# Token mixes from one shared difference, ten plain-float32 attention heads instead of twelve, and a first q that ScalarE loads and rounds

## The chip, the cores and the metric

The kernel runs on one core of a Trainium2 chip. The metric is the device time of one execution in microseconds (us); lower is better. The engines are called PE (TensorE matmuls), PEld (TensorE weight loads), DVE (VectorE), ACT (ScalarE), POOL (GpSimd) and SP (SyncE, which here issues the DMAs).

## What the kernel computes

Four sequences ("batches") of 448 tokens with 12 heads of 64 channels go through sigmoid attention, a gated layer that mixes each token with the one before it, and a token and channel mixer. Everything is float32.

```python
scores = scale * q @ k.T - log(S);  attn = sigmoid(scores);  x = attn @ v          # per batch and head
x_prev = x shifted by one token (zeros first)
xk = mu_k * x + (1 - mu_k) * x_prev;   xr = mu_r * x + (1 - mu_r) * x_prev
k = relu(xk @ w_k);   v = k*k @ w_v;   r = sigmoid(xr @ w_r);   x = r * v
h = relu(x.T @ w_tok1) @ w_tok2;       u = x + h.T
out = u + relu(u @ w_ch1) @ w_ch2
```

## The kernel before

**Precision.** A float32 matrix is split into a high part, rounded to the fast format float32r, and a low part, the rest (`split`, L97 to L102): one cast on ACT or DVE (L99 or L101) and one subtract, always on DVE (L102). A product of two split matrices is three matmuls, L409, L411 and L412 of `products`. An attention head multiplies its scores with v either split or plain. A split head has, for each half of its scores `a`, a cast `ah` on ACT (L211) and subtracts on DVE (L215 for the first half, L217 and L218 for the second), then 7 matmuls (L235, L237), an ACT copy (L239) and a DVE add (L240) into `xe`; its v is split too. A plain head has 4 matmuls in plain float32 (L230, recorded as 8) and one ACT copy (L231), and nothing on DVE. `NATIVE` (L51) names the plain heads as (batch, head): 8 of batch 0, 4 of batch 1.

**The mix.** `xe` holds x with a column of zeros ahead, channels on partitions, in six blocks of 128 channels by 448 tokens. `mix_unit` does one block for one of the two mixes: x_prev times (1 - mu) (L396 on ACT, or L398 on DVE for batch 2), mu times x plus that (L399 on DVE), and a split of the result into `Ah` and `Al`. Which engine takes a cast is in `ONDVE` (L38).

**The stages.** Batch 0's attention runs first. Then `first_part(b)` runs for batch 0 (products with w_r, six column blocks; with w_k, eight; with w_v, six of two chunks each; then the token mixer), with the attention of batch 1 spread between its matmuls, then `first_part` of batch 1, then `second_part` for both (w_ch1, w_ch2). The same again for batches 2 and 3. Weights arrive in a raw 8-byte format on their first use (L308), are narrowed by two ACT (L273, L275) and two DVE instructions (L278, L281), stored (L322), and split into `whi` (ACT, L99) and `wlo` (DVE, L102); a matmul chunk can't start its L412 before its `wlo`. On later uses they are loaded narrowed. Raw tiles have 2 buffers, split weights 3, PSUM tiles of the products 3.

**Order.** The work is written out in units (attention, mixes, weights), but a scheduler at build time sets the order on each engine; each engine then runs its own list strictly in that order. The very first loads are issued by SP (`load_k`, `load_q`, `load_v`), and the first head's q is split by DVE.

Of the kernel before, what the change touches and what calls it, by code (L numbers as in the profile page):

```python
# [22 lines left out]
P = 128  # L23
NT = C // P
# [10 lines left out]
    return ap.bitcast(F32)  # L35


ONDVE = [('K', 0), ('K', 1), ('K', 2), ('K', 3), ('Q', 0), ('Q', 2), ('Q', 3), ('V', 1), ('V', 2), ('kk', 0), ('kk', 3), ('mix', 1), ('mix', 2), ('mix', 3), ('prev', 2), ('sq', 2)]  # L38


WARM = 12
# [6 lines left out]

NATIVE = {(0, 1), (0, 7), (0, 4), (1, 1), (0, 3), (1, 8), (1, 4), (0, 6), (0, 2), (0, 5), (1, 9), (0, 11)}  # L51


def native(b, pr, h):
# [4 lines left out]
def kernel(  # L59
# [34 lines left out]
    def ENG(kind, b):  # L94
        return DVE if (kind, b) in ONDVE else ACT

# [12 lines left out]
    def load_k(g):  # L109
        if g < B * NPAIR:  # L110
            kns[g] = a2.tile([P, 4 * P], F32, tag="kn", name="kn")
            SP.dma_start(out=kns[g], in_=k[g])

    def load_q(g):
        if g < B * H:
            qns[g] = a3.tile([P, S], F32, tag="qn", name="qn")
            SP.dma_start(out=qns[g], in_=q[g])

    def load_v(g):
        if g < B * NPAIR:  # L120
            vns[g] = a2.tile([P, 2, 4, D], F32, tag="vn", name="vn")
            SP.dma_start(out=vns[g], in_=v[g])


    warm = const.tile([P, 1], F32, tag="warm", name="warm")
    DVE.memset(warm, 0.0)
# [5 lines left out]
    for _ in range(WARM):  # L132
        PE.matmul(idle[:, :S], zero[:, :P], zero, start=True, stop=True)

    load_k(0)
    load_q(0)
    load_v(0)
    load_q(1)

# [4 lines left out]
    load_q(2)  # L144
    load_v(1)

    mus = {}
    for name, src in (("k", mu_k), ("r", mu_r)):
        m = const.tile([P, NT], F32, tag="mu" + name, name="mu" + name)
        SP.dma_start(out=m, in_=src)  # L150
        om = const.tile([P, NT], F32, tag="om" + name, name="om" + name)
        DVE.tensor_scalar(out=om, in0=m, scalar1=-1.0, scalar2=1.0, op0=ALU.mult, op1=ALU.add)
        mus[name] = (m, om)


    xe = big.tile([P, NT, 1 + S], F32, tag="xe", name="xe")
# [15 lines left out]
    def unit_q(b, pr, h):  # L172
        g = b * NPAIR + pr
        st = att[(b, pr, h)]
        qn = qns.pop(2 * g + h)
        Q1 = a2.tile([P, S], F32R, tag="Q1", name="Q1")
        Q2 = a2.tile([P, S], F32R, tag="Q2", name="Q2")
        split(Q1, Q2, qn, ENG("Q", b))
        st["Q"] = (Q1, Q2)
        load_q(2 * g + h + 3)  # L180
        vn = vns[g][:, h]
        if native(b, pr, h):
            st["v"] = vn
        else:
            vs = a3.tile([P, 4, 2 * D], F32R, tag="vs", name="vs")
            split(vs[:, :, 0:D], vs[:, :, D:], vn, ENG("V", b))
            st["v"] = vs
        if h == 1:
            load_v(g + 2)
# [198 lines left out]
    def col(p, t):  # L388
        return p[:, t * S : (t + 1) * S]

    def mix_unit(name, t, dst, b):
        m, om = mus[name]
        t1 = tmps.tile([P, S], F32, tag="tmp", name="mix1")
        t2 = tmps.tile([P, S], F32, tag="tmp", name="mix2")
        if ENG("prev", b) is ACT:
            ACT.activation(t1, xe[:, t, 0:S], AF.Copy, scale=om[:, t : t + 1])  # L396
        else:
            DVE.tensor_scalar(out=t1, in0=xe[:, t, 0:S], scalar1=om[:, t : t + 1], scalar2=None, op0=ALU.mult)  # L398
        DVE.scalar_tensor_tensor(  # L399
            out=t2, in0=xe[:, t, 1:], scalar=m[:, t : t + 1], in1=t1, op0=ALU.mult, op1=ALU.add  # L400
        )
        split(col(dst[0], t), col(dst[1], t), t2, ENG("mix", b))


    def products(ps, n, count, parts, stacked=None):
# [19 lines left out]
    def new_mm():  # L425
        return ps_mm.tile([P, 512], F32, tag="mm", name="psmm")

    def first_part(b, xr, xk, rows, u):
        rows[:] = [big.tile([P, S], F32, tag="r%d" % m, name="r%d" % m) for m in range(NT)]


        for m in range(NT):
            ps = new_mm()
            yield from products(ps, S, NT, chunked(1, NT, xr))
            ACT.activation(rows[m], ps[:, :S], AF.Sigmoid)


        kk = pair_tiles("M", 12 * S)
        for m in range(F // P):
            ps = new_mm()  # L440
            yield from products(ps, S, NT, chunked(1, NT, xk))
            t1 = tmps.tile([P, S], F32, tag="tmp", name="k1")
            t2 = tmps.tile([P, S], F32, tag="tmp", name="k2")
            ACT.activation(t1, ps[:, :S], AF.Relu)
            if ENG("sq", b) is ACT:
                ACT.activation(t2, t1, AF.Square)
            else:
                DVE.tensor_tensor(out=t2, in0=t1, in1=t1, op=ALU.mult)
            split(col(kk[0], m), col(kk[1], m), t2, ENG("kk", b))

        yt = xk_tiles()
        ytv = [t.rearrange("p (r c) -> p r c", r=4) for t in yt]

        def y_transpose(m):
            ps = new_mm()
            psv = ps.rearrange("p (r c) -> p r c", r=4)
            ms = slice(m * P, (m + 1) * P)
            for r in range(4):  # L460
                n = P if r < 3 else TAIL
                PE.transpose(psv[:n, r], rows[m][:, r * P : r * P + n], ident)  # L462
            hi, lo = (t[:, :, ms] for t in ytv)
            split(hi[:, :3], lo[:, :3], psv[:, :3], ACT)
            split(hi[:TAIL, 3], hi[TAIL:, 3], psv[:TAIL, 3], ACT)

        for m in range(NT):
            ps = new_mm()
            for i, cost in enumerate(products(ps, S, 8, chunked(2, 4, kk))):
                yield cost  # L470
                if i == 1 and m:
                    y_transpose(m - 1)
            DVE.tensor_tensor(out=rows[m], in0=rows[m], in1=ps[:, :S], op=ALU.mult)


        h1v = [t[:, : 2 * C].rearrange("p (j c) -> p j c", j=2) for t in pair_tiles("M", 12 * S)]
        wt1 = []
        for half in range(2):
            cs = slice(half * HC, (half + 1) * HC)
            for j in range(TOK // P):  # L480
                if half == 0:
                    wt1.append(weights())
                    wst["hold"] = j == 1
                wh, wl = wt1[j]
                ps = new_mm()
                yield from products(ps, HC, 4, [(wh[:, r], wl[:, r], *(t[:, r, cs] for t in ytv)) for r in range(4)], 3)
                if half == 0 and j == 0:
                    y_transpose(NT - 1)
                ACT.activation(h1v[0][:, j, cs], ps[:, :HC], AF.Relu)
                DVE.scalar_tensor_tensor(  # L490
                    out=h1v[1][:, j, cs],
                    in0=ps[:, :HC],
                    scalar=0.0,
                    in1=f32(h1v[0][:, j, cs]),
                    op0=ALU.max,
                    op1=ALU.subtract,
                )
        wst["hold"] = False
        w_tick()
        if b % 2:  # L500
            u[:] = u_tiles()
        for m in range(NT):
            ps = new_mm()
            ms = slice(m * P, (m + 1) * P)
            yield from products(
                ps, S, 2, ((h1v[0][:, j, ms], h1v[1][:, j, ms], wt2h[:, j], wt2l[:, j]) for j in range(2))
            )
            DVE.tensor_tensor(out=rows[m], in0=rows[m], in1=ps[:, :S], op=ALU.add)
            if b % 2 == 0:
                SP.dma_start(out=away[m], in_=rows[m])  # L510
            else:
                t1 = tmps.tile([P, S], F32, tag="tmp", name="back")
                SP.dma_start(out=t1, in_=away[m])
                split(u[0][:, m, :S], u[1][:, m, :S], t1, ACT)
                split(u[0][:, m, S:], u[1][:, m, S:], rows[m], ACT)
# [39 lines left out]
                    SP.dma_start(out=out[b0 + 1, m * P : (m + 1) * P], in_=rows[m])  # L555


    def mix_units(name, box, b):
        def mix(t):
            if t == 0:  # L560
                box[name] = xk_tiles() if name == "k" else xr_tiles()
            mix_unit(name, t, box[name], b)

        return [lambda t=t: mix(t) for t in range(NT)]

    box = {}
    for i, unit in enumerate(attention_units(0, [mix_units("r", box, 0), mix_units("k", box, 0)])):
        unit()
        if i == TOK2:
            load_tok2()  # L570
            w_raw(1)
        if i == EARLY:
            w_ready(1)
# [6 lines left out]
    def spread(units, start, end):  # L580
        return [(start + (end - start) * i / len(units), f) for i, f in enumerate(units)]

    now, todo = 0.0, []
    rows, u = [], []

    def run(gen):
# [6 lines left out]
    for b in range(0, B, 2):  # L593
        nxt = {}
        todo += spread(attention_units(b + 1, [mix_units("r", nxt, b + 1)]), now, now + END_1 * t_a)
        run(first_part(b, box["r"], box["k"], rows, u))
        todo += spread(mix_units("k", nxt, b + 1), now + 0.01 * t_a, now + 0.12 * t_a)
        box = {}
        if b + 2 < B:
# [3 lines left out]
            todo += spread(mix_units("k", box, b + 2), t0 + 0.87 * t_c, t0 + 0.97 * t_c)  # L603

        def second_batch():
            while "r" not in nxt or "k" not in nxt:
                todo.pop(0)[1]()
            yield from first_part(b + 1, nxt["r"], nxt["k"], rows, u)

        run(second_batch())  # L610
        run(second_part(b, rows, u))
# [77 lines left out]
```

## Time and profile before

| | before |
|---|---|
| median of 3 runs | 942.76 us (942.66 to 944.78) |
| the profiled execution | 942.98 us, span 941.1 us |
| PE, PEld busy | 930.5 us (99%), 806.3 us (86%) |
| DVE, ACT busy | 661.2 us (70%), 517.3 us (55%) |
| granted TensorE clock, mean | 0.998 |

Busy shares are averages over the whole span; the stages differ. Matmuls are pipelined and their ends are modelled, so two matmul rows overlap by more than half their length: what one costs is the distance from its start to the next start. To a smaller extent this holds for the other engines too.

### The profile page before, as it was taken

The page shows a single profiled execution, that of the slowest core. Times are in us where ns is not written, and L with a number is a line of the kernel's source. Part 1 is how long each engine was busy: PE and PEld are TensorE (multiplying, and loading weights), DVE is VectorE, ACT ScalarE, POOL GpSimd, SP SyncE. Part 2 cuts the span into 40 slices and gives each one's busy share as a digit, 9 for nine tenths or more (in the row PEclk, how much of TensorE's full clock was granted, in tenths as well). Part 3 has the DMA queues.
Part 4 walks back from the last instruction along what each step waited for, and adds up shares of the span by engine and source line. Part 5 has one row for each costly group of instructions (what it writes and reads, how often), then busy time and mean ns, then how long its engine had stood idle before and what let it go on. Part 6 is the DMA issues. An engine that isn't in the chain of part 4 may idle for free.

```text
span 941.1 us, 12125 instructions
## 1 busy us (share of the span) xinstructions
PE 930.5 (99%) x4472; PEld 806.3 (86%) x4472; DVE 661.2 (70%) x1111; ACT 517.3 (55%) x794; POOL 1.2 (0%) x8
## 2 busy tenths in 40 slices
PE   8999999999999999999999999999999999999998
PEld 4476788779998988998988999999999998889987
DVE  8999899989567988777789478988745552323231
ACT  6998989674774767546641367767444342112210
POOL 0000000000000000000000000000000000000000
PEclk9999999999999999999999999999999999999999
DMA  7646665775344465555544333323334321232131
GB/s 240 219 134 235 233 222 192 229 231 167 118 134 139 131 223 202 194 186 185 188 144 157 123 109 116 109 63 99 106 106 151 115 80 51 90 124 71 51 110 62
DMA packets 57083, 137.38 MB, mean 146 GB/s; under 512 B 6592, under 2 KB 23488, under 8 KB 57024
## 3 DMA queue, kind: packets, MB, share of 16 engines
q1 hardware_dynamic: 57024, 136.61, 44.9%
q8 instruction: 35, 0.57, 0.3%
q14 instruction: 24, 0.20, 0.1%
HBM read 106.96 MB, written 29.62 MB: 145 GB/s over the span
## 4 chain that ended last, share of the span: by engine, by line
PE 90%; DVE 4%; DMA 3%; ACT 2%; issue 0%; SPq 0%; ACTq 0%; DVEq 0%
PE psmm L412 25%; PE psmm L409 25%; PE psmm L411 25%; PE psc L197 3%; PE psc L198 3%; PE pav L230 3%; PE pav L235 3%; PE pav L237 2%; DMA raw<-in_moe_w_k_dram 1%; PE psmm L462 1%; DVE wd L278 1%; ACT wd L273 1%; DMA raw<-in_moe_w_r_dram 1%; DMA w<-wd 1%; DVE KK L102 0%
## 5 line engine op out<-in xcount | busy, mean ns | idle before, releaser
L409 PE MATMUL psmm<-Ah,whi 128*128 128x448 f32 (+2 forms) x688 | 250.0, 364 | 1.9 <-ACT whi L99 1.9
L412 PE MATMUL psmm<-Ah,wlo 128*128 128x448 f32 (+2 forms) x688 | 250.9, 365 | 0.6 <-DVE wlo L102 0.6
L99 ACT CAST whi<-wd 128x768 fp32r<-128x768 f32 (+1 forms) x160 | 121.4, 759 | 225.0 <-PE psmm L411 204.8
L411 PE MATMUL psmm<-Al,whi 128*128 128x448 f32 (+2 forms) x672 | 244.7, 364 | 0.1
L102 DVE TENSOR_TENSOR wlo<-wd,whi 128x768 fp32r<-128x768 f32 (+1 forms) x160 | 137.8, 862 | 93.8 <-ACT whi L99 88.8
L409 PE MATMUL psmm<-Mh,whi 128*128 128x448 f32 (+2 forms) x480 | 176.4, 368 | 0.2 <-ACT whi L99 0.2
L412 PE MATMUL psmm<-Mh,wlo 128*128 128x448 f32 (+2 forms) x480 | 176.0, 367 | 0.0
L411 PE MATMUL psmm<-Ml,whi 128*128 128x448 f32 (+2 forms) x480 | 175.1, 365 | 0.0
L409 PEld LDWEIGHTS psmm<-Ah,whi 128*128 128x128 f32 x688 | 129.6, 188 | 18.3 <-ACT whi L99 2.7
L412 PEld LDWEIGHTS psmm<-Ah,wlo 128*128 128x128 f32 x688 | 129.5, 188 | 14.4 <-DVE wlo L102 2.0
L411 PEld LDWEIGHTS psmm<-Al,whi 128*128 128x128 f32 x672 | 126.4, 188 | 12.7 <-DVE Al L102 0.6
L204 ACT ACTIVATE a<-psc 128x896 f32<-128x896 f32 x96 | 87.2, 917 | 32.0 <-PE psc L198 30.4
L412 PEld LDWEIGHTS psmm<-Mh,wlo 128*128 128x128 f32 x480 | 90.1, 188 | 11.8 <-DVE wlo L102 1.6
L409 PEld LDWEIGHTS psmm<-Mh,whi 128*128 128x128 f32 x480 | 90.2, 188 | 11.0 <-ACT whi L99 0.8
L411 PEld LDWEIGHTS psmm<-Ml,whi 128*128 128x128 f32 x480 | 90.2, 188 | 8.8
L197 PE MATMUL psc<-Q,KK 128*128 128x448 f32 x192 | 71.9, 375 | 0.4 <-ACT a L204 0.4
L198 PE MATMUL psc<-Q,KK 128*128 128x448 f32 x192 | 70.6, 369 | 0.7 <-DVE Q L102 0.7
L211 ACT CAST ah<-a 128x896 fp32r<-128x896 f32 x72 | 67.7, 944 | 1.0
L278 DVE SCALAR_TENSOR_TENSOR wd<-wd,raw 128x768 uint32<-128x768 uint32 (+2 forms) x54 | 47.1, 874 | 16.4 <-ACT wd L273 8.6
L273 ACT ACTIVATE wd<-raw 128x768 f32<-128x768 f32 (+2 forms) x54 | 45.1, 835 | 24.3 <-DVE wlo L102 10.4
L536 DVE SCALAR_TENSOR_TENSOR Ml<-psmm,Mh 128x512 fp32r<-128x512 f32 (+1 forms) x48 | 29.8, 621 | 34.7 <-ACT Mh L535 34.6
L235 PE MATMUL pav<-ah,vs 128*128 128x448 f32 x144 | 53.3, 370 | 0.0
(79 smaller groups left out, 1051.6 us busy)
## 6 DMA issues: line engine op xcount, KB each, us to landing
wd<-w SPq DMA_DIRECT2D x66, 384.0 KB, 3.0
raw<-in_moe_w_ch_dram SPq DMA_DIRECT2D x24, 768.0 KB, 4.8
w<-wd SPq DMA_DIRECT2D x38, 384.0 KB, 2.6
qn<-in_q_dram SPq DMA_DIRECT2D x48, 224.0 KB, 2.9
wd<-w SPq DMA_DIRECT2D x42, 256.0 KB, 2.7
kn<-in_k_dram SPq DMA_DIRECT2D x24, 256.0 KB, 2.9
vn<-in_v_dram SPq DMA_DIRECT2D x24, 256.0 KB, 3.1
raw<-in_moe_w_k_dram SPq DMA_DIRECT2D x8, 768.0 KB, 5.6
```

The lines of the kernel that those rows point to most:

```text
L99: ACT.copy(hi, src)
L102: DVE.tensor_tensor(out=lo, in0=src, in1=f32(hi), op=ALU.subtract)
L197: PE.matmul(ps[:, j, :S], K[:, c * P : (c + 1) * P], Q1, start=True, stop=False)
L198: PE.matmul(ps[:, j, :S], K[:, c * P : (c + 1) * P], Q2, start=False, stop=True)
L204: ACT.activation(a, ps[:, :, :S], AF.Sigmoid, bias=-math.log(S), scale=1.0 / math.sqrt(D))
L211: ACT.copy(ah, a)
L235: PE.matmul(ps[:, :S], vs[:, c], ah[:, c % 2], start=(c == 0), stop=(c == 3))
L273: ACT.activation(f32(dst), f32(hi), AF.Copy, scale=2.0**-112)
L278: DVE.scalar_tensor_tensor(out=dst, in0=dst, scalar=3, in1=lo, op0=ALU.logical_shift_left, op1=ALU.bitwise_or)
L409: PE.matmul(ps[:, :n], wh, xh, start=(i == 0), stop=False)
L411: PE.matmul(ps[:, :n], wh, xl, start=False, stop=False)
L412: PE.matmul(ps[:, :n], wl, xh, start=False, stop=(i == count - 1))
```

## The change

Three edits. (1) `NATIVE` loses heads (1, 1) and (0, 11), which become split heads. (2) `mix_r` forms one difference x - x_prev per block on DVE; then two DVE instructions add (mu - 1) times it to x, once for r into a temporary and once for k, in place in `xe`; each is split as before. ACT's scaled copies (L396) are gone, and with them L398. Batch 1's cast of the mixed block goes from DVE to ACT. Batch 0's k splits become units of their own that are written into the beginning of `first_part(0)`. (3) The first q is loaded by an ACT-issued DMA, placed with the first k ahead of the warm-up, and its cast goes from DVE to ACT.

```diff
-ONDVE = [... ('mix', 1), ('mix', 2), ('mix', 3), ('prev', 2), ('sq', 2)]
+ONDVE = [... ('mix', 2), ('mix', 3), ('sq', 2)]
-NATIVE = {(0, 1), (0, 7), (0, 4), (1, 1), (0, 3), (1, 8), (1, 4), (0, 6), (0, 2), (0, 5), (1, 9), (0, 11)}
+NATIVE = {(0, 1), (0, 7), (0, 4), (0, 3), (1, 8), (1, 4), (0, 6), (0, 2), (0, 5), (1, 9)}
-            SP.dma_start(out=qns[g], in_=q[g])
+            (SP if g else ACT).dma_start(out=qns[g], in_=q[g])
-        split(Q1, Q2, qn, ENG("Q", b))
+        split(Q1, Q2, qn, ENG("Q", b) if 2 * g + h else ACT)
-        DVE.tensor_scalar(out=om, in0=m, scalar1=-1.0, scalar2=1.0, op0=ALU.mult, op1=ALU.add)
+        DVE.tensor_scalar(out=om, in0=m, scalar1=-1.0, scalar2=None, op0=ALU.add)
-    def mix_unit(name, t, dst, b):
-        if ENG("prev", b) is ACT:
-            ACT.activation(t1, xe[:, t, 0:S], AF.Copy, scale=om[:, t : t + 1])
-        else:
-            DVE.tensor_scalar(out=t1, in0=xe[:, t, 0:S], scalar1=om[:, t : t + 1], scalar2=None, op0=ALU.mult)
-        DVE.scalar_tensor_tensor(
-            out=t2, in0=xe[:, t, 1:], scalar=m[:, t : t + 1], in1=t1, op0=ALU.mult, op1=ALU.add
-        )
+    def mix_r(t, dst, b):
+        DVE.tensor_tensor(out=d, in0=xe[:, t, 1:], in1=xe[:, t, 0:S], op=ALU.subtract)
+        for name, to in (("r", t2), ("k", xe[:, t, 1:])):
+            DVE.scalar_tensor_tensor(
+                out=to, in0=d, scalar=less[name][:, t : t + 1], in1=xe[:, t, 1:], op0=ALU.mult, op1=ALU.add
+            )
         split(col(dst[0], t), col(dst[1], t), t2, ENG("mix", b))
+    def mix_k(t, dst, b):
+        split(col(dst[0], t), col(dst[1], t), xe[:, t, 1:], ENG("mix", b))
+        if b == 0:
+            todo += spread(mix_units("k", box, 0), now + 0.01 * t_a, now + 0.15 * t_a)
```

**The start.** This is ACT's list from its beginning, before and then after. The first rows are the table load and a dummy activation; `qn` is a raw q, `Q` a split one, `a` the sigmoid scores.

```order
L127 ACT_TABLE_LOAD
L127 ACTIVATE warm<-warm 128x1
L99 CAST vs<-vn 128x4x64
L204 ACTIVATE a<-psc 128x896 x2
L211 CAST ah<-a 128x896 x2
```

```order
L117 DMA qn<-in_q_dram 128x448
L129 ACT_TABLE_LOAD
L129 ACTIVATE warm<-warm 128x1
L99 CAST Q_211<-qn 128x448
L99 CAST vs<-vn 128x4x64
L204 ACTIVATE a<-psc 128x896 x2
L211 CAST ah<-a 128x896 x2
```

The load of q and its cast now stand on ACT; the load is ahead of the table load, the cast ahead of the first cast of v.

**The end of batch 0's attention.** This is DVE's list from the `wlo` of the fifth w_r chunk to that of the sixth, before and then after. `Al<-xe` is the low part of a k mix, `al<-a,ah` that of a split head's scores, `wd` a weight being narrowed.

```order
L102 TENSOR_TENSOR wlo<-wd,whi 128x768
L102 TENSOR_TENSOR vs<-vn,vs 128x4x64
L278 SCALAR_TENSOR_TENSOR wd<-wd,raw 128x768
L102 TENSOR_TENSOR KK<-kn,KK 64x512
L281 SCALAR_TENSOR_TENSOR wd<-raw,wd 128x768
L278 SCALAR_TENSOR_TENSOR wd<-wd,raw 128x768
L101 CAST vs<-vn 128x4x64
L281 SCALAR_TENSOR_TENSOR wd<-raw,wd 128x768
L102 TENSOR_TENSOR wlo<-wd,whi 128x768
```

```order
L102 TENSOR_TENSOR wlo<-wd,whi 128x768
L215 TENSOR_TENSOR al<-a,ah 128x896
L240 TENSOR_TENSOR xe<-pav,avt 64x448
L102 TENSOR_TENSOR Al<-xe,Ah 128x448
L278 SCALAR_TENSOR_TENSOR wd<-wd,raw 128x768
L102 TENSOR_TENSOR Q_966<-qn,Q_965 128x448
L281 SCALAR_TENSOR_TENSOR wd<-raw,wd 128x768
L101 CAST vs<-vn 128x4x64
L101 CAST KK<-kn 64x512
L102 TENSOR_TENSOR vs<-vn,vs 128x4x64
L102 TENSOR_TENSOR KK<-kn,KK 64x512
L102 TENSOR_TENSOR wlo<-wd,whi 128x768
```

Between the two `wlo` there is now one weight narrowed instead of two, and in the other's place the subtract and the add of a head that is now split, a k split that was earlier, and parts of the next head.

## Rows read from the trace of the kernel before

**Rows 1.** The page, busy time (share of the span) and instructions of each engine.
```profile
PE 930.5 (99%) x4472; PEld 806.3 (86%) x4472; DVE 661.2 (70%) x1111; ACT 517.3 (55%) x794; POOL 1.2 (0%) x8
```

**Rows 2.** Busy time by stretch; the first row names the columns.
```profile
core 0: us, PE busy (x) PEld busy (x) DVE busy (x) ACT busy (x) POOL busy (x), PEclk, DMA share, GB/s
3.36:189.70 186.34, 181.46 (x753) 129.64 (x751) 175.71 (x300) 158.00 (x244) 0.00 (x0) 0.99 0.65 215
189.70:231.20 41.50, 41.26 (x198) 35.08 (x197) 38.09 (x71) 26.15 (x42) 0.00 (x0) 1.00 0.62 202
600.00:700.00 100.00, 100.00 (x506) 91.82 (x505) 76.16 (x132) 59.20 (x95) 0.00 (x0) 1.00 0.31 94
700.00:800.00 100.00, 100.00 (x511) 91.56 (x510) 48.66 (x83) 38.76 (x71) 0.00 (x0) 1.00 0.33 100
```

**Rows 3.** Timeline, DVE and PE: a w_v chunk's wlo and its first L412, twice.
```profile
156.50 0.68 DVE L102 TENSOR_TENSOR wlo<-wd,whi 128x512 fp32r<-128x512 f32 x1
157.25 0.47 PE L412 MATMUL psmm<-Mh,wlo 128*128 128x448 f32 x1
...
188.98 0.69 DVE L102 TENSOR_TENSOR wlo<-wd,whi 128x512 fp32r<-128x512 f32 x1
189.59 0.55 DVE L102 TENSOR_TENSOR Al<-psmm,Ah 128x384 fp32r<-128x384 f32 x1
190.11 0.47 PE L412 MATMUL psmm<-Mh,wlo 128*128 128x448 f32 x1
```

**Rows 4.** Timeline, DVE: its longest waits behind 3.36 us, in brackets.
```profile
39.10 0.96 DVE L278 SCALAR_TENSOR_TENSOR wd<-wd,raw 128x768 uint32<-128x768 uint32 x1 [1.04 <-ACT raw L275]
95.97 0.96 DVE L278 SCALAR_TENSOR_TENSOR wd<-wd,raw 128x768 uint32<-128x768 uint32 x1 [3.19 <-ACT raw L275]
197.35 0.69 DVE L278 SCALAR_TENSOR_TENSOR wd<-wd,raw 128x512 uint32<-128x512 uint32 x1 [2.89 <-ACT wd L273]
```

**Rows 5.** Timeline, PE: plain head (0, 11), then a split head's first and last of 7.
```profile
71.16 3.36 PE L230 MATMUL pav<-a,vn 128*64 128x448 f32 x8
74.45 0.47 PE L197 MATMUL psc<-Q,KK 128*128 128x448 f32 x1
...
75.37 0.36 PE L235 MATMUL pav<-ah,vs 128*128 128x448 f32 x1
...
76.58 0.36 PE L235 MATMUL pav<-ah,vs 128*128 128x448 f32 x1
76.78 0.36 PE L197 MATMUL psc<-Q,KK 128*128 128x448 f32 x1
```

**Rows 6.** Timeline, DVE and PE: the start.
```profile
3.36 0.87 DVE L101 CAST KK<-kn 64x512 fp32r<-64x512 f32 x2 [2.50 <-DMA kn<-in_k_dram]
4.98 0.39 DVE L101 CAST Q<-qn 128x448 fp32r<-128x448 f32 x1
5.43 0.70 PE L197 MATMUL psc<-Q,KK 128*128 128x448 f32 x2
```

**Rows 7.** Groups by line: shapes, count, busy us, mean ns of one, idle before.
```profile
L215 DVE TENSOR_TENSOR al<-a,ah 128x896 fp32r<-128x896 f32 x36 | 39.2, 1088 | 11.9 <-ACT ah L211 11.7
L102 DVE TENSOR_TENSOR KK<-kn,KK 64x512 fp32r<-64x512 f32 x48 | 32.9, 686 | 1.5
L102 DVE TENSOR_TENSOR Al<-mix,Ah 128x448 fp32r<-128x448 f32 x48 | 29.7, 621 | 0.4
L101 DVE CAST KK<-kn 64x512 fp32r<-64x512 f32 x48 | 20.1, 418 | 3.2 <-DMA kn<-in_k_dram 2.5
L399 DVE SCALAR_TENSOR_TENSOR mix<-xe,mur,mix 128x448 f32<-128x448 f32 x24 | 16.3, 681 | 1.0 <-ACT mix L396 0.7
L102 DVE TENSOR_TENSOR vs<-vn,vs 128x256 fp32r<-128x256 f32 x36 | 15.1, 421 | 0.5
L101 DVE CAST Ah<-mix 128x448 fp32r<-128x448 f32 x36 | 14.0, 390 | 0.5
L396 ACT ACTIVATE mix<-xe,omr 128x448 f32<-128x448 f32 x18 | 12.0, 668 | 3.8 <-DVE xe L240 3.6
```

More of the change, by code (lines that the diff above doesn't have):

```diff
@@ L35, in f32 @@
     return ap.bitcast(F32)
-ONDVE = [('K', 0), ('K', 1), ('K', 2), ('K', 3), ('Q', 0), ('Q', 2), ('Q', 3), ('V', 1), ('V', 2), ('kk', 0), ('kk', 3), ('mix', 1), ('mix', 2), ('mix', 3), ('prev', 2), ('sq', 2)]
+ONDVE = [('K', 0), ('K', 1), ('K', 2), ('K', 3), ('Q', 0), ('Q', 2), ('Q', 3), ('V', 1), ('V', 2), ('kk', 0), ('kk', 3), ('mix', 2), ('mix', 3), ('sq', 2)]
 WARM = 12
@@ L122, in load_v @@
             SP.dma_start(out=vns[g], in_=v[g])
+    load_k(0)
+    load_q(0)
     warm = const.tile([P, 1], F32, tag="warm", name="warm")
@@ L133 @@
         PE.matmul(idle[:, :S], zero[:, :P], zero, start=True, stop=True)
-    load_k(0)
-    load_q(0)
     load_v(0)
@@ L145 @@
     load_v(1)
-    mus = {}
+    less = {}
     for name, src in (("k", mu_k), ("r", mu_r)):
@@ L151 @@
         om = const.tile([P, NT], F32, tag="om" + name, name="om" + name)
-        DVE.tensor_scalar(out=om, in0=m, scalar1=-1.0, scalar2=1.0, op0=ALU.mult, op1=ALU.add)
-        mus[name] = (m, om)
+        DVE.tensor_scalar(out=om, in0=m, scalar1=-1.0, scalar2=None, op0=ALU.add)
+        less[name] = om
     xe = big.tile([P, NT, 1 + S], F32, tag="xe", name="xe")
@@ L389, in col @@
         return p[:, t * S : (t + 1) * S]
-    def mix_unit(name, t, dst, b):
-        m, om = mus[name]
-        t1 = tmps.tile([P, S], F32, tag="tmp", name="mix1")
-        t2 = tmps.tile([P, S], F32, tag="tmp", name="mix2")
-        if ENG("prev", b) is ACT:
-            ACT.activation(t1, xe[:, t, 0:S], AF.Copy, scale=om[:, t : t + 1])
-        else:
-            DVE.tensor_scalar(out=t1, in0=xe[:, t, 0:S], scalar1=om[:, t : t + 1], scalar2=None, op0=ALU.mult)
-        DVE.scalar_tensor_tensor(
-            out=t2, in0=xe[:, t, 1:], scalar=m[:, t : t + 1], in1=t1, op0=ALU.mult, op1=ALU.add
-        )
+    def mix_r(t, dst, b):
+        d = tmps.tile([P, S], F32, tag="tmp", name="diff")
+        t2 = tmps.tile([P, S], F32, tag="tmp", name="mixr")
+        DVE.tensor_tensor(out=d, in0=xe[:, t, 1:], in1=xe[:, t, 0:S], op=ALU.subtract)
[3 more added lines that the diff above has]
+            )
         split(col(dst[0], t), col(dst[1], t), t2, ENG("mix", b))
+    def mix_k(t, dst, b):
+        split(col(dst[0], t), col(dst[1], t), xe[:, t, 1:], ENG("mix", b))
     def products(ps, n, count, parts, stacked=None):
@@ L426, in new_mm, with first_part @@
         return ps_mm.tile([P, 512], F32, tag="mm", name="psmm")
-    def first_part(b, xr, xk, rows, u):
+    def first_part(b, box, rows, u):
         rows[:] = [big.tile([P, S], F32, tag="r%d" % m, name="r%d" % m) for m in range(NT)]
+        xr = need(box, "r")
         for m in range(NT):
@@ L435, in first_part @@
             ACT.activation(rows[m], ps[:, :S], AF.Sigmoid)
+        xk = need(box, "k")
         kk = pair_tiles("M", 12 * S)
@@ L555, in second_part, with need @@
                     SP.dma_start(out=out[b0 + 1, m * P : (m + 1) * P], in_=rows[m])
+    todo = []
+    def need(box, name):
+        while name not in box or box[name][0] < NT:
+            todo.pop(0)[1]()
+        return box[name][1]
     def mix_units(name, box, b):
@@ L560, in mix @@
             if t == 0:
-                box[name] = xk_tiles() if name == "k" else xr_tiles()
-            mix_unit(name, t, box[name], b)
+                box[name] = [0, xk_tiles() if name == "k" else xr_tiles()]
+            (mix_r if name == "r" else mix_k)(t, box[name][1], b)
+            box[name][0] += 1
         return [lambda t=t: mix(t) for t in range(NT)]
     box = {}
-    for i, unit in enumerate(attention_units(0, [mix_units("r", box, 0), mix_units("k", box, 0)])):
+    for i, unit in enumerate(attention_units(0, [mix_units("r", box, 0)])):
         unit()
@@ L581, in spread @@
         return [(start + (end - start) * i / len(units), f) for i, f in enumerate(units)]
-    now, todo = 0.0, []
+    now = 0.0
     rows, u = [], []
@@ L595 @@
         todo += spread(attention_units(b + 1, [mix_units("r", nxt, b + 1)]), now, now + END_1 * t_a)
-        run(first_part(b, box["r"], box["k"], rows, u))
+        if b == 0:
+            todo += spread(mix_units("k", box, 0), now + 0.01 * t_a, now + 0.15 * t_a)
+            todo.sort(key=lambda x: x[0])
+        run(first_part(b, box, rows, u))
         todo += spread(mix_units("k", nxt, b + 1), now + 0.01 * t_a, now + 0.12 * t_a)
@@ L605, in second_batch @@
         def second_batch():
-            while "r" not in nxt or "k" not in nxt:
-                todo.pop(0)[1]()
-            yield from first_part(b + 1, nxt["r"], nxt["k"], rows, u)
+            yield from first_part(b + 1, nxt, rows, u)
         run(second_batch())
```

## Prediction

> **What bounds the kernel now.** I read the page first: PE is recorded busy for 99% of the span [rows 1], so it looks as if only less matmul work could help. Then I read the busy time by stretch, which says otherwise for the first fifth. From DVE's first cast at 3.36 us to the end of the `wlo` of the last w_v chunk at 189.70 us, DVE works 175.71 of 186.34 us, 94%; from 600 to 800 us it has 24% and then 51% to spare [rows 2]. So the early stretch has two nearly full engines, and the late ones only PE.
>
> Which of the two waits in the early stretch is read from the timeline at the weight chunks. A `wlo` ends at 156.50 + 0.68 = 157.18 us, and the first matmul that needs it starts at 157.25. At the last w_v chunk the `wlo` ends at 189.67 and its matmul starts at 190.11, with other matmuls put in between [rows 3]. PE takes each chunk almost as DVE hands it over. DVE's list is strictly in order, so a `wlo` ends no earlier than everything ahead of it in that list, and PE, in order too, can't pass the matmul that waits. I therefore use that last `wlo` as a **mark**: what comes out later there comes out later at the end, unless PE finds waits behind the mark to give back.
>
> The trace supports a reading by weight loads: they fill only 129.64 us of the stretch, 70%, against 181.46 us of recorded matmuls [rows 2]. The Trainium skill, "Trainium Kernel Development and Optimization", section Performance Expectations, says that recorded matmul time is a bad measure, because matmuls are pipelined, and that the weight loads' share is a good one. By matmul time the change would give back all the PE work that it removes; by that rule PE has room here and the gain may be lost to another engine. The trace agrees, as [rows 3] show a matmul waiting in a stretch recorded as busy, though plain heads load few weights and lower that share as well.
>
> **The change on PE.** A plain head holds PE from 71.16 to 74.45 us, 3.29 us; the 7 matmuls of a split head take 75.37 to 76.78, 1.41 us [rows 5]. Two heads change: 2 x 1.88 = 3.8 us less PE work. All other matmuls are the same, in another order.
>
> **The start.** The first score matmul waits for DVE's cast of q, 4.98 to 5.43 us [rows 6]. With the cast on ACT, whose list has only a table load ahead of it, it can start when DVE's k is done, about 4.98: 0.4 us if q has landed by then, 0 if not. I take 0.4, and DVE loses one cast. SP's remaining first loads move up by one place, which nothing waits for; ACT's table load moves back by one DMA issue, and its next work is the cast of q.
>
> **The change on DVE.** Adjacent DVE rows overlap: the row at 188.98 is 0.69 long and the next starts 0.61 later [rows 3]. So I price each instruction at its mean [rows 7] less 0.08 us. That gives 0.54 for a two-input instruction of 448 columns (the Al row; L217, L218 and L240 are of the same kind), 0.60 for L399, 1.01 for L215, 0.31 for a cast of 448, 0.34 for v's subtract, 0.34 and 0.61 for a K cast and subtract.
>
> Up to the mark, DVE's list of the changed kernel differs from that of before by this count:
>
> - 10 differences (6 blocks of batch 0, 4 of batch 1): 10 x 0.54 = 5.4
> - 20 multiply-adds instead of 16: 4 x 0.60 = 2.4. Four of these are for the k mix of batch 1, whose rows stood behind the mark until now
> - two heads more that are split: 2 x (1.01 + 3 x 0.54) = 5.3
> - one v subtract more, 0.3; one K cast and subtract, moved behind the mark, -0.95
> - five casts fewer (4 of batch 1's mix, 1 of q): -1.55
>
> The sum is +10.9 us on 16 more rows. The difference is not in the trace of before. Its price lies between that of a cast (0.31) and of L399 (0.60), so the sum lies between 8.6 and 11.5; with two full inputs it is nearest to the Al subtract. The in-place multiply-add has L399's shape; I let it share that spread. The single-input cast at 390 ns beside the two-input subtract at 621 ns, both of 448 columns, shows that merging the scaled copies into a subtract buys no cheap instruction [rows 7]. The Trainium skill, "VectorE: DVE Perf Modes", section The perf-mode tier table, has float32 tensor_tensor at 1x and single-input operations at 2x, which speaks against this edit in the same way; the rows agree. Priced at 2x the sum would be 8.6.
>
> What the edit buys is ACT time: 12 scaled copies of batch 0 and the first four of batch 1, 0.67 us each [rows 7], while two split heads and batch 1's casts put some back. ACT is at 158.00 of 186.34 us in the stretch [rows 2], so it isn't the engine that lacks time. The k splits of batch 0 (a cast and a subtract each) are not saved but moved; five of the six now stand after the r splits and among the narrowing of weights, as the second place of the order shows.
>
> Behind the mark the count evens out or is covered: batch 3 gains a difference per block, 6 x 0.54 = 3.2 us at most, where DVE has 24% to 51% to spare [rows 2], and batch 2 loses two copies for one difference. If that cover were gone it would cost those 3.2 us.
>
> **The sum.** DVE's work up to the mark becomes 175.71 + 10.9 = 186.6 us, and it can't start before 3.36: 189.97 us, already 0.3 later than the mark of before (189.70), without a single wait. DVE had 10.63 us of waits in that stretch [rows 2]; how many stay is the open term. Two large ones, 1.04 and 3.19 [rows 4], were on ACT's half of the narrowing, the second behind a raw weight load. With ACT lighter and the narrowing spread out they can go: that leaves 6.4. The rest are short handovers, and I take 6.0. Bounds: 3, if half of those go too, and 10.6, if all return. Behind the mark PE can regain something, where DVE waited 2.89 us for a weight at 197.35 [rows 4]: between 0 and 2.9, and I take half, 1.4. PE's remaining work there is what it was, since both heads are done by then.
>
> So 942.98 + 0.3 + 6.0 - 1.4 = 947.9 us against the profiled execution's own 942.98; the median of the runs shown is 0.2 lower, so **947.6 us**. PE's saved 4.2 us is gone into waits: it arrives earlier at each chunk and waits longer for it.
>
> **The rivals.** *PE's work decides (faster).* If PE is held by its own matmuls and a `wlo` that ends just in time is only good scheduling, the whole PE saving counts: 942.98 - 3.8 - 0.4 = 938.8, so 938.6. For it: 99% busy [rows 1] and few long waits. Against: the list of DVE must then fit 186.6 us of work into about 182. It decides once DVE's instructions ahead of the mark are some 4 us cheaper than their rows.
>
> *DVE absorbs it (no change).* Waits fall to 0 to 3 us and PE regains 1.4: 942.98 + 0.3 - 1.4 = 941.9 to 944.9, so about 943. For it: DVE's waits are mostly on others, and others got lighter. Against: a share of 98% or more of an in-order list that depends on ACT and on loads.
>
> *The weights come late as well (much slower).* The k splits stand between the narrowing instructions, a raw buffer is freed later, the next load and the 3.19 us wait return, and PE regains nothing: 942.98 + 0.3 + 10.6 = 953.9.
>
> **How the numbers follow.** About 0.3%, 2.8 us, is what a measurement of this kernel can tell from no change. I give the forecast's mechanism, 945.6 to 952.5 us, a chance of 0.55, the late weights above that 0.07, no change (940 to 945.6) 0.25, and PE's work 0.13. So slower 0.62, same 0.25, faster 0.13. The likeliest case's own range is 944 to 951. The 8-in-10 range reaches from 940.5, which leaves nearly all of the faster case out, to 952.5.
>
> **What would show it.** In the profile of the changed kernel, DVE's busy share from 3.4 us to the last w_v `wlo` should be 96 to 98% instead of 94%, that `wlo` should end at 194 to 197 us, and the waits of PE's L409 and L412 for `whi` and `wlo` between 80 and 190 us should grow by 8 to 10 us. The first score matmul should start near 5.0 us, the plain heads should be 80 rows, and the stretch behind 231 us should take as long as before. I would be wrong if the `wlo` of the last w_v chunk ends before 188 us, if the difference rows are much shorter than 0.6 us, or if PE still loses time behind 231 us, where nothing here should reach.

## The result

The changed kernel takes 951.52 us in the median of 4 runs (950.38 to 953.08), the kernel before 943.32 us beside it (942.66 to 944.78, 4 runs). The ratio is 1.0086 with a 95% interval of 1.0069 to 1.0103: about 8.2 us slower, near the upper end of the range given. The profiled execution took 951.33 us, span 949.5 us, at a mean granted clock of 0.999.

The page of the changed kernel, busy time by engine, answers to [rows 1]:

```profile
PE 929.0 (98%) x4470; PEld 804.0 (85%) x4470; DVE 670.6 (71%) x1121; ACT 507.4 (53%) x776; POOL 1.2 (0%) x8
```

PE works less, ACT works less, and only DVE works more, by 9.4 us. Where that matters shows in the busy time by stretch, cut at the same work as [rows 2]: from DVE's first cast to the end of the `wlo` of the last w_v chunk (the mark), and 41.5 us behind it. The columns are those of [rows 2].

```profile
4.14:198.90 194.76, 179.92 (x748) 127.23 (x747) 186.76 (x316) 156.17 (x238) 0.00 (x0) 1.00 0.61 202
198.90:240.40 41.50, 41.04 (x197) 34.87 (x196) 37.53 (x68) 25.00 (x42) 0.00 (x0) 1.00 0.65 211
600.00:700.00 100.00, 100.00 (x506) 91.58 (x505) 79.73 (x140) 54.74 (x87) 0.00 (x0) 1.00 0.32 99
700.00:800.00 100.00, 100.00 (x512) 92.18 (x511) 51.99 (x88) 40.77 (x75) 0.00 (x0) 1.00 0.36 104
```

The mark falls at 198.90 instead of 189.70 us: 9.2 us late, and the whole execution is 8.35 us late (951.33 against 942.98). So all of the loss is there by the mark, and 0.85 us come back behind it. DVE's work ahead of the mark rose from 175.71 to 186.76 us, 11.05 us, with 316 instructions instead of 300; its waits fell from 10.63 to 8.00 us.

PE now waits for weights more often and longer. The timeline of the changed kernel at the last w_v chunk answers to [rows 3]:

```profile
196.98 0.62 ACT L99 CAST whi<-wd 128x512 fp32r<-128x512 f32 x1 [0.44 <-DVE wd L281]
197.65 0.19 PEld L411 LDWEIGHTS psmm<-Mh,whi 128*128 128x128 f32 x1 [1.60 <-ACT whi L99]
197.65 0.47 PE L411 MATMUL psmm<-Mh,whi 128*128 128x448 f32 x1 [1.22 <-ACT whi L99]
...
198.24 0.68 DVE L102 TENSOR_TENSOR wlo<-wd,whi 128x512 fp32r<-128x512 f32 x1
199.56 0.47 PE L414 MATMUL psmm<-Mh,wlo 128*128 128x448 f32 x1
```

ACT's `whi` itself waited for DVE's narrowing (L281), PE for the `whi`. The line L414 is the L412 of before, L411 the L409. The list of waits of PE's weight loads from 80 to 190 us (total us, times, longest) shows the same. These are its two largest groups apart from issue before, and then its largest in the changed kernel:

```profile
PEld psmm L409 <- ACT whi L99: 3.1, 3, 2.3
PEld psmm L412 <- DVE wlo L102: 2.3, 6, 0.7
```

```profile
PEld psmm L414 <- DVE wlo L102: 6.6, 11, 1.2
PEld psmm L411 <- ACT whi L99: 4.2, 9, 1.3
PEld psc L198 <- DVE Q L102: 3.2, 2, 2.1
PEld pav L235 <- DVE ah L218: 1.9, 5, 0.6
```

Weights are only a part of it. The waits of PE itself from DVE's first cast to the mark are, before, all that the list has, and in the changed kernel the first four of eleven groups:

```profile
PE psmm L409 <- ACT whi L99: 2.2, 2, 1.9
PE pav L237 <- DVE al L215: 0.9, 1, 0.9
PE psc L198 <- DVE Q L102: 0.7, 1, 0.7
PE psc L197 <- ACT a L204: 0.4, 1, 0.4
PE psmm L412 <- DVE wlo L102: 0.3, 1, 0.3
```

```profile
PE psmm L414 <- DVE wlo L102: 3.3, 7, 0.8
PE psc L198 <- DVE Q L102: 2.5, 2, 1.7
PE psmm L411 <- ACT whi L99: 2.5, 3, 1.2
PE pav L237 <- DVE al L215: 1.8, 2, 1.5
```

Summed over all groups, PE's waits for DVE grew from 1.9 to 11.2 us, those for ACT from 2.6 to 3.5. So it is DVE that PE now waits for, and more for the low parts of q, k and the scores (5.8 us) than for weights (3.3).

DVE's own longest waits in the stretch, in the timeline of the changed kernel, answer to [rows 4]; the 3.19 us wait for a raw weight is down to 0.74:

```profile
101.04 0.96 DVE L278 SCALAR_TENSOR_TENSOR wd<-wd,raw 128x768 uint32<-128x768 uint32 x1 [0.74 <-ACT raw L275]
142.63 0.96 DVE L102 TENSOR_TENSOR wlo<-wd,whi 128x768 fp32r<-128x768 f32 x1 [1.04 <-ACT whi L99]
...
195.32 0.69 DVE L278 SCALAR_TENSOR_TENSOR wd<-wd,raw 128x512 uint32<-128x512 uint32 x1 [1.58 <-ACT raw L275]
```

The start answers to [rows 6]:

```profile
4.14 0.88 DVE L101 CAST KK<-kn 64x512 fp32r<-64x512 f32 x2 [3.27 <-DMA kn<-in_k_dram]
4.32 0.57 ACT L99 CAST Q<-qn 128x448 fp32r<-128x448 f32 x1 [1.65 <-DMA qn<-in_q_dram]
5.88 0.70 PE L197 MATMUL psc<-Q,KK 128*128 128x448 f32 x2
6.44 0.47 PE L198 MATMUL psc<-Q,KK 128*128 128x448 f32 x1
```

The first k lands 0.78 us later than before, now that the first q is loaded at the same moment, and the first scores start 0.45 us later, not 0.4 earlier. But the next score matmul comes 0.37 us earlier than before, where it waited for DVE's low part of q:

```profile
6.81 0.47 PE L198 MATMUL psc<-Q,KK 128*128 128x448 f32 x1 [0.68 <-DVE Q L102]
```

The groups by line of the changed kernel give the prices that [rows 7] could only bound: the difference costs what the subtract of the Al row costs, the in-place multiply-add what L399 cost.

```profile
L398 DVE SCALAR_TENSOR_TENSOR mixr<-diff,omr,xe 128x448 f32<-128x448 f32 x24 | 16.3, 679 | 0.2
L398 DVE SCALAR_TENSOR_TENSOR xe<-diff,omk,xe 128x448 f32<-128x448 f32 x24 | 16.3, 678 | 0.1
L396 DVE TENSOR_TENSOR diff<-xe 128x448 f32<-128x448 f32 x24 | 14.8, 619 | 0.4 <-DMA p<-z 0.3
```

### The profile page after: what moved, and what is told of

It reads as the page before. It is cut to its first block, busy times and chain, and to the rows that moved or that the text cites. A ratio compares the mean times of both kernels' runs of the same rounds, so it can differ in the third digit from the quotient of the medians.

```text
span 949.5 us, 12120 instructions
## 1 busy us (share of the span) xinstructions
PE 929.0 (98%) x4470; PEld 804.0 (85%) x4470; DVE 670.6 (71%) x1121; ACT 507.4 (53%) x776; POOL 1.2 (0%) x8
## 4 chain that ended last, share of the span: by engine, by line
PE 84%; DVE 8%; DMA 4%; ACT 3%; issue 1%; SPq 0%; ACTq 0%; DVEq 0%
PE psmm L414 24%; PE psmm L411 23%; PE psmm L413 23%; PE pav L230 3%; PE psc L197 3%; PE psc L198 3%; PE pav L235 2%; DMA raw<-in_moe_w_v_dram 2%; PE pav L237 2%; PE psmm L466 1%; DVE wd L278 1%; DVE wlo L102 1%; DVE wd L281 1%; DMA raw<-in_moe_w_k_dram 1%; DVE KK L102 1%
## 5 line engine op out<-in xcount | busy, mean ns | idle before, releaser
L414 PE MATMUL psmm<-Ah,wlo 128*128 128x448 f32 (+2 forms) x688 | 250.2, 364 | 2.4 <-DVE wlo L102 2.4
L411 PE MATMUL psmm<-Ah,whi 128*128 128x448 f32 (+2 forms) x688 | 249.6, 364 | 1.3 <-ACT whi L99 1.3
L411 PE MATMUL psmm<-Mh,whi 128*128 128x448 f32 (+2 forms) x480 | 176.7, 368 | 1.2 <-ACT whi L99 1.2
L414 PE MATMUL psmm<-Mh,wlo 128*128 128x448 f32 (+2 forms) x480 | 175.9, 367 | 1.0 <-DVE wlo L102 1.0
L414 PEld LDWEIGHTS psmm<-Ah,wlo 128*128 128x128 f32 x688 | 129.1, 188 | 17.4 <-DVE wlo L102 4.8
L411 PEld LDWEIGHTS psmm<-Ah,whi 128*128 128x128 f32 x688 | 129.0, 188 | 15.9 <-ACT whi L99 3.7
L414 PEld LDWEIGHTS psmm<-Mh,wlo 128*128 128x128 f32 x480 | 90.1, 188 | 12.6 <-DVE wlo L102 2.4
L411 PEld LDWEIGHTS psmm<-Mh,whi 128*128 128x128 f32 x480 | 90.2, 188 | 12.4 <-ACT whi L99 2.4
L211 ACT CAST ah<-a 128x896 fp32r<-128x896 f32 x76 | 71.4, 943 | 1.1
L235 PE MATMUL pav<-ah,vs 128*128 128x448 f32 x152 | 56.9, 374 | 1.4 <-ACT ah L211 0.5
```

Source lines behind the costliest of these rows:

```text
L211: ACT.copy(ah, a)
L235: PE.matmul(ps[:, :S], vs[:, c], ah[:, c % 2], start=(c == 0), stop=(c == 3))
L411: PE.matmul(ps[:, :n], wh, xh, start=(i == 0), stop=False)
L414: PE.matmul(ps[:, :n], wl, xh, start=False, stop=(i == count - 1))
```

## The experiments

Theory: up to the mark the amount of work in DVE's in-order list sets the time, once its waits are used up. Rivals: PE's own matmuls set it; or it is not the amount but the order of weights, or the longer chains of split heads, or ACT. Each run was timed beside the kernel before on the same chip; the first four shared one session, the next four another, the last four a third. In the table "mark" is the end of the last w_v chunk's `wlo` in the profiled execution, "work" and "waits" are DVE's busy and idle time from its first cast to there. All of it is read from the busy time by stretch of each run. A difference "by the ratio" is one of these ratios, or of two of them, turned into us; it allows for differences between sessions.

| run | mark | DVE work | DVE waits | median us | ratio to before (95%) |
|---|---|---|---|---|---|
| before | 189.7 | 175.7 | 10.6 | 942.5 to 943.3 | 1 |
| e7: 14 plain heads | 191.0 | 170.3 | 17.2 | 944.36 | 1.0017 (1.0004 to 1.0030) |
| e3: first q alone | 190.2 | 175.3 | 10.7 | 942.66 | 1.0004 (0.9994 to 1.0015) |
| e4: changed, 12 heads | 190.9 | 180.2 | 6.7 | 942.18 | 0.9998 (0.9988 to 1.0009) |
| e5: before, 10 subtracts more | 189.3 | 180.4 | 5.4 | 945.65 | 1.0027 (1.0015 to 1.0039) |
| e2: mix alone | 190.6 | 180.5 | 6.7 | 941.92 | 0.9995 (0.9983 to 1.0006) |
| e10: e4, difference on POOL | 192.3 | 180.9 | 7.2 | 948.33 | 1.0066 (1.0053 to 1.0078) |
| e1: heads alone | 192.7 | 182.2 | 7.1 | 943.90 | 1.0025 (1.0014 to 1.0037) |
| e12: changed, 11 heads | 195.1 | 183.2 | 7.9 | 948.07 | 1.0061 (1.0040 to 1.0081) |
| e6: changed, q casts on ACT | 199.0 | 183.8 | 10.9 | 950.64 | 1.0080 (1.0063 to 1.0096) |
| e11: e4, 10 subtracts more | 198.8 | 185.8 | 9.1 | 948.77 | 1.0068 (1.0055 to 1.0080) |
| changed | 198.9 | 186.8 | 8.0 | 951.52 | 1.0086 (1.0069 to 1.0103) |
| e8: changed, first q by SP | 200.0 | 186.9 | 9.6 | 951.85 | 1.0088 (1.0072 to 1.0103) |
| e9: changed, difference on POOL | 198.4 | 187.1 | 7.3 | 954.03 | 1.0124 (1.0108 to 1.0139) |

The profiled executions also differ in something that the table doesn't show, the granted clock. In that of the kernel before, PE waits 1.94 us for a `whi` just ahead of 113.20 us, and soon after the clock is at 1.2 instead of 2.4 GHz:

```profile
110.00:114.60 4.60, 2.35 (x12) 1.50 (x10) 3.86 (x8) 4.30 (x7) 0.00 (x0) 1.00 0.66 210
114.60:118.00 3.40, 3.40 (x9) 3.05 (x10) 3.40 (x6) 3.28 (x5) 0.00 (x0) 0.50 0.73 240
```

Matmuls start 0.37 us apart there instead of 0.21, so up to 1.7 us of the time of before (half of 3.4, an estimate) may be the clock's. Ahead of the mark, e3 and e9 have one such stretch, e6 one from 76.7 to 83.5 us, e8 and e12 two each; the other eight executions have none. The profiled executions of e3, e6 and e8 were also the slowest of their runs (944.05, 952.60 and 953.88 us). So the marks are comparable only to within some 2 us, and those of e6, e8 and e12 less well.

**e1, the heads alone.** On the kernel before:

```diff
-NATIVE = {(0, 1), (0, 7), (0, 4), (1, 1), (0, 3), (1, 8), (1, 4), (0, 6), (0, 2), (0, 5), (1, 9), (0, 11)}
+NATIVE = {(0, 1), (0, 7), (0, 4), (0, 3), (1, 8), (1, 4), (0, 6), (0, 2), (0, 5), (1, 9)}
```

> The kernel before with heads (1,1) and (0,11) split, nothing else. Theory (DVE's in-order list sets the first 200 us): DVE work ahead of the last w_v wlo grows by 6.2 us, of which about a quarter is taken out of DVE's waits: +4.7 us, near 948 us. Rival (PE's own work decides): 3.8 us less PE work, near 939.5 us. Rival (only the mix edit costs): no change.

It is 2.4 us slower by the ratio: with 3.8 us less PE work, so PE's own work is not what decides. (The medians alone, 943.90 and 942.65, differ by 1.25 us.) About half of the cost forecast is absent, as the waits gave more (3.5 of 6.4 us) than the quarter assumed.

**e2, the mix alone.** The changed kernel with the old `NATIVE`, and the first q loaded and split as before.

> The changed kernel with its mix, but the 12 plain heads and the first q as before. Theory: DVE work ahead of the last w_v wlo is 5.6 us more than before: +4.2 us, near 947.5 us, with PE's work as before. Rival (PE's own work decides, and ACT's relief helps): no change or up to 2 us faster.

No difference, so the theory's number was wrong here. DVE's work at the mark is up by 4.7 us, where 5.6 were expected, and its waits gave back 4.0 of them. The busy time by stretch of this run, columns as above:

```profile
3.47:190.60 187.13, 182.01 (x754) 127.77 (x753) 180.45 (x306) 153.22 (x234) 0.00 (x0) 1.00 0.64 213
```

**e3, the first q alone.** On the kernel before:

```diff
-            SP.dma_start(out=qns[g], in_=q[g])
+            (SP if g else ACT).dma_start(out=qns[g], in_=q[g])
-        split(Q1, Q2, qn, ENG("Q", b))
+        split(Q1, Q2, qn, ENG("Q", b) if 2 * g + h else ACT)
```

(and the first two loads ahead of the warm-up).

> The kernel before with the first q loaded by an ACT-issued DMA beside the first k and cast on ACT, nothing else. Theory: the first k lands 0.8 us later because the two loads share the DMA engines, DVE saves a cast of 0.3: +0.5 us. Rival (the prediction's own step): the first scores start 0.4 us earlier, -0.4 us.

No difference that can be measured. DVE starts at 4.16 us, as in the changed kernel. The interval, -0.6 to +1.4 us, holds both times expected, so this run doesn't decide between them.

**e4, the 12 heads back.** The changed kernel with the old `NATIVE`.

> The changed kernel with 12 plain heads again. Theory: 5.7 us of DVE work less ahead of the last w_v wlo, 3.8 us more PE work that fits into PE's waits: about 4.3 us faster than the changed kernel, near 947 us. Rival (PE's own work decides): 3.8 us slower than the changed kernel, near 955 us.

Everything is back: 942.18 us. The same two heads that cost 2.4 us on the kernel before cost 8.3 us by the ratio on top of the mix edit (9.3 by the medians). Busy time by stretch of e4, beside the first row of the changed kernel above: 6.6 us less DVE work, and the mark 8.0 us earlier.

```profile
4.04:190.90 186.86, 181.81 (x753) 127.83 (x751) 180.15 (x305) 154.03 (x235) 0.00 (x0) 1.00 0.63 212
```

**e5 and e11, a dose of DVE work.** The same addition to the kernel before and to e4; it repeats a subtract of the r mix with the same operands and result. This is e4's; in the kernel before, where one function does both mixes, the condition also has `name == "r"`:

```diff
         split(col(dst[0], t), col(dst[1], t), t2, ENG("mix", b))
+        if b == 0 or b == 1 and t < 4:
+            DVE.tensor_tensor(out=col(dst[1], t), in0=t2, in1=f32(col(dst[0], t)), op=ALU.subtract)
```

> The kernel before with the low-part subtract of ten r mix blocks (six of batch 0, four of batch 1) done twice on DVE, the second time with the same operands and result; nothing computed differs. Theory (amount of DVE work): 10 x 0.54 = 5.4 us more DVE work, 4.8 us of it more at the last w_v wlo: +3.6 us or more, near 947 us. Rival (it is the new order of weights and loads, or the split heads' longer chains, not the amount of DVE work): under 1 us.

> The changed kernel with 12 plain heads and ten r-mix subtracts done twice, as in the run of the kernel before with ten subtracts more. Theory (the mix edit has used up DVE's spare waits): 5.3 us more DVE work cost 4 to 5 us, near 946.5 us, more than the 3 us they cost on the kernel before. Rival (waits absorb as much here as there): 3 us or less, 945 us or under.

On the kernel before the dose costs 2.5 us by the ratio; on e4, which is as fast, it costs 6.6 us (948.77 against 942.18, from two sessions whose kernels before agree at 942.65). The first is under the number expected, the second over it. No split head and no other work was added, so longer chains of split heads are not needed for the loss, and the price of the dose depends on how much DVE has already. The order is not held fixed, though: the scheduler at build time orders anew, and of e4's 305 DVE instructions ahead of the mark at most 224 stand in the same order in e11. So these two runs don't exclude that a part of the price is the order's. In e5 the waits fell from 10.6 to 5.4 us; in e11 they gave nothing and rose from 6.7 to 9.1:

```profile
3.93:198.80 194.87, 183.66 (x755) 127.89 (x754) 185.82 (x315) 154.58 (x236) 0.00 (x0) 1.00 0.62 204
```

In e5 the mark is no later at all, but its execution has no stretch at the low clock and that of before has one. It took 943.97 us, 1.0 more than that of before and 1.7 less than its own run's median, so it shows only a part of the 2.5 us. Where that part arises is seen at equal work: the `wlo` of the same weights are 1.0 us late at 107 us, 2.0 early at 130, behind the low clock of before, and 0.9 late again at 300 us and at the end.

**e12, one head.** The changed kernel with (1, 1) plain again, so 11 plain heads.

> The changed kernel with head (1,1) plain again: 11 plain heads. Theory (1:1 with DVE work): DVE work ahead of the last w_v wlo lies 2.5 us over that with 12 heads and 3.2 us under that with 10, so about 946 us, between 942.2 and 951.5. Rival (one of the two heads alone brings the loss): 942 or 951 us.

948.07 us, between the two: by the ratio, splitting (0, 11) costs 5.9 us over e4, and (1, 1) 2.4 on top of it (a runs' spread of 945.8 to 952.4 leaves this rough). So (0, 11) alone doesn't bring the whole loss, and the single-head rival is not met; that (1, 1) alone would bring some of it was not run.

**e6, q casts on ACT.** The changed kernel without `('Q', 0)` in `ONDVE`.

> The changed kernel with the eleven remaining q casts of batch 0 on ACT instead of DVE. Theory: 3.4 us less DVE work ahead of the last w_v wlo, 11 x 0.57 = 6.3 us more ACT work, which ACT has room for: about 2.5 us faster than the changed kernel, near 949 us. Rival (ACT's chain from a raw weight to whi sets the time): 1 to 5 us slower than the changed kernel.

A miss: 0.6 us faster than the changed kernel by the ratio, which is within the noise. DVE has 2.9 us less work ahead of the mark, and the mark is where it was, since its waits grew by 2.9 us. Casts take 0.57 us on ACT instead of 0.39 on DVE, and ACT has 4.5 us more to do in the stretch, 160.67 us. That DVE's saved work came back as waits for ACT fits this but isn't shown, since the profiled execution ran from 76.7 to 83.5 us at the low clock and took 2.0 us more than the median:

```profile
4.26:199.00 194.74, 180.46 (x748) 129.62 (x747) 183.81 (x305) 160.67 (x249) 0.00 (x0) 0.98 0.62 203
```

**e7, 14 plain heads.** The kernel before with (0, 8) and (1, 2) plain too.

> The kernel before with two more plain heads, (0,8) and (1,2): 14. DVE work ahead of the last w_v wlo falls by 6.6 us, PE work grows by 3.8 us. Theory (DVE sets the early stretch in the kernel before too): no slower than before, between -3 and +1 us. Rival (PE's own work decides in the kernel before): +3.8 us, near 947 us.

1.6 us slower by the ratio, a miss between the two times expected: DVE has 5.4 us less work and simply waits 6.6 us more, while PE's idle time is what it was (4.6 us, 4.9 before). So the kernel before stands about where PE's work and DVE's work meet: two plain heads fewer cost 2.4 us by DVE, and two more cost 1.6, most likely by PE.

**e8, the first q by SP.** The changed kernel with `SP.dma_start` for every q, the cast of the first still on ACT.

> The changed kernel with the first q loaded by SP behind the first k, its cast still on ACT. Theory: the first k lands 0.8 us earlier again, DVE starts at 3.4 us instead of 4.1: 0.5 to 0.8 us faster than the changed kernel. Rival: no difference, the start is covered later.

DVE starts at 3.58 instead of 4.14 us and the time can't be told from that of the changed kernel. The 0.5 to 0.8 us expected are less than these runs can tell, so that the start is covered is likely and not shown.

**e9 and e10, the difference on POOL.** The changed kernel and e4 with one word changed:

```diff
-        DVE.tensor_tensor(out=d, in0=xe[:, t, 1:], in1=xe[:, t, 0:S], op=ALU.subtract)
+        POOL.tensor_tensor(out=d, in0=xe[:, t, 1:], in1=xe[:, t, 0:S], op=ALU.subtract)
```

> The changed kernel with the difference of the mix formed on POOL instead of DVE (ACT's work unchanged). Theory (amount of DVE work, 1:1 once its waits are used up): 4.9 us less DVE work ahead of the last w_v wlo: 4 to 5 us faster than the changed kernel, near 947 us. Rival (what lost the time is the longer chain of the split heads or later weights): under 1.5 us faster. If POOL's subtract holds DVE up or takes several us, no gain either, and the trace shows it.

> The changed kernel with 12 plain heads and the difference on POOL: DVE work ahead of the last w_v wlo 0.7 us under that of the kernel before, ACT work far under it. Theory: DVE's work stops to matter below about 180 us of work at that point, PE's own matmuls take over: 0 to 2 us faster than with the difference on DVE, 940 to 942 us. Rival (DVE's work counts 1:1 throughout): 6 us faster, near 936 us.

Both are slower than with the difference on DVE, by 3.6 and 6.4 us by the ratio (2.5 and 6.1 by the medians), which neither theory nor rival forecast; only for e9 was it named that POOL might hold DVE up. The trace shows why this is no test of the theory: DVE's instructions fell from 316 to 308 ahead of the mark, but its work stayed at 187.1 us. The timeline of e9 shows a DVE cast (the third row) that took 1.04 us beside POOL's subtract, where its kind takes 0.42:

```profile
40.06 0.39 DVE L101 CAST Q<-qn 128x448 fp32r<-128x448 f32 x1
40.29 0.95 POOL L396 TENSOR_TENSOR diff<-xe 128x448 f32<-128x448 f32 x1 [9.63 <-ACT xe L231]
40.48 1.04 DVE L101 CAST KK<-kn 64x512 fp32r<-64x512 f32 x1
41.55 0.69 DVE L398 SCALAR_TENSOR_TENSOR mixr<-diff,omr,xe 128x448 f32<-128x448 f32 x1
```

This doesn't explain why they are slower. The loss arises behind the mark, where DVE has less work than with the difference on DVE: e9's mark is 0.5 us earlier than the changed kernel's and its profiled end 2.4 later; e10's mark is 1.4 later than e4's and its end 6.5. The cause of that stays open.

No run beat the kernel before: e2 and e4 can't be told from it.

## Why the prediction was right

**What bounds.** Right: the mark moved by 9.2 us and the end by 8.35. e1, e4 and e11 show that more DVE work ahead of the mark brings the loss and less takes it away, and that PE's 3.8 us are not kept: with 10 heads PE's recorded matmuls fill 179.92 of 194.76 us instead of 181.46 of 186.34. The reading by weight loads pointed the right way, at 65% now (127.23 of 194.76) against 70%. "PE takes each chunk almost as DVE hands it over" was read from two chunks; from 80 to 190 us it holds, to within 0.1 us, for 10 of 23 weights before and for 15 of 21 in the changed kernel.

**The signs.** The plain heads are 80 rows, the difference takes 0.62 us, and the time from 41.5 us behind the mark on is 709.1 us against 709.9, as said. The rest was missed in size: DVE's share up to the mark is 95.9% (96 to 98 were forecast), the mark is at 198.90 us (194 to 197), the weight loads' waits for `whi` and `wlo` from 80 to 190 us grew by 5.4 us, from 5.4 to 10.8 (8 to 10), and the first score matmul started at 5.88 us (5.0). The time itself, 951.52 us, is inside the range, 3.9 us above the 947.6 forecast and 0.5 above the likeliest case's own 944 to 951.

**PE's saving and DVE's work.** The work was sized well: +10.9 us forecast, +11.05 measured, on 16 more instructions. The difference took 619 ns, the Al row 621, so the end of the bound that was taken held, and by the 2x price the sum would have been off by 2.3 us. The 7 matmuls of a split head are priced by their starts, 0.20 us apart; their rows are 0.36 long, so they overlap by a little under half, and not by more than half.

**The start.** Wrong for the first scores: 0.4 us earlier was forecast, and they come 0.45 later, as DVE starts 0.78 us later. The gain comes one step further on, where the next score matmul is 0.37 us ahead. Neither e3 nor e8 shows an effect on the time, and neither could tell one under 1 us.

**The open term.** The waits that stay were taken as 6.0 us and were 8.00. Together with the later start and the regained 0.85 instead of 1.4 this is the 3.4 us between the 4.9 us of the sum and the 8.35 measured: 0.78 + 0.15 + 2.0 + 0.55, less 0.1 of rounding. This is the term that was mis-sized: both long waits on ACT's half of the narrowing were to go, 4.2 us. The largest shrank from 3.19 to 0.74, but up to the mark DVE still waited 2.7 us for raw weights (4.4 before) and 1.0 for a `whi`. The rest of the 8.00 us are shorter handovers, most of which stayed.

**What the sum missed.** It treats the three edits as if each added its share. They don't add: alone they cost 2.4 us and twice nothing that can be told, together 8.2. For single edits the same theory expected 4.2 us of e2, which cost nothing, and 4.7 of e1, which cost 2.4; so that its sum for all three came as near as 4.9 of 8.35 us is in part luck. In the table the mark stays between 189 and 193 us for 170 to 182 us of DVE work, and beyond that it rises by 1.2 us for each us of work (from e4 to the changed kernel, 8.0 for 6.6; neither has a stretch at the low clock). The other runs with over 180 us of work, with orders of their own, lie within about 1 us of that line, except e5 (1.9 us early) and e6 (3.7 late), and that speaks for the amount of work more than for the order. DVE's 10.6 us of waits hold about 5 us of reserve; the mix edit alone uses it up and so looks free, and the two heads then pay in full.

**The rivals.** That DVE absorbs it is what happens to each edit alone, not to all. That PE's work decides is refuted by e1 and e4, for 12 heads and fewer; with 14 it seems to (e7). That the weights come late with 10.6 us of waits came close in its time (953.9), but not in its way: DVE's wait at that raw load fell to 0.74 us.

**Still open.** Why the mark rises by more than the work beyond 182 us, and why e6 gets nothing for 2.9 us less: the two in-order lists of DVE and ACT wait for each other there, but beyond the heads no run took work away without giving it to ACT or POOL. What the order alone costs is open too, as no run kept the amount of work and changed the order.

## What to carry to other kernels

Where two engines are both nearly full in one stretch, count the work ahead of a point that all engines pass, in the order in which the program is built, and compare it with the time of that point: the engine whose work no longer fits sets it, whatever the busy shares over the whole span are. An edit that costs nothing alone may have used up the waits that a second edit needs, so such edits are timed together and apart. Work saved on the engine that only waits is worth nothing.

## What was not expected of the hardware

A subtract of 128x448 float32 on POOL took 1.2 us and slowed DVE: a cast that takes 0.42 us took 1.04 us beside it. In e9, 8 of the 18 DVE instructions that ran beside the ten subtracts ahead of the mark took 0.4 to 0.7 us longer than their kind in the changed kernel, 5.3 us in all, of the 6.2 that the ten had taken on DVE. And the first k landed later when the first q was issued at the same moment from another queue: DVE's first cast began at 3.36 to 3.58 us in the six kernels in which SP issues the q behind the k, and at 3.93 to 4.26 in the eight in which ACT issues it.
